# Merging neighbouring VectorE instructions of a frequency-domain mixer, and moving its bias transposes and its gelu table

## The chip, the cores and the metric

The kernel runs on one core of one Trainium2 chip. A core has TensorE (PE in the profile, with its weight loads as PEld), VectorE (DVE), ScalarE (ACT), GpSimd (POOL), and SyncE (SP), which here only issues transfers. The engines run their own instruction streams in order and meet through semaphores. The metric is the device time of one execution in microseconds (us). Before the change it is 179.74 us, the median of three runs (179.69 to 180.02).

## The reference, cut to what matters

Two branches are computed from the same input x = A_q (2048 positions, 640 channels), and a gate per position mixes them:

```python
g = sigmoid((x * gate_w).sum(-1))
# branch a: causal convolution over the 2048 positions, by FFT of length 4096
kv = (k shifted by 4 taps, weighted with shift_k) * v
y  = irfft(rfft(kv, 4096) * rfft(ssm_k, 4096))[:2048] + kv * ssm_D
a  = x * y
# branch b: a token MLP
h  = layernorm(x)
u  = gelu(h^T @ w1 + b1)        # 640 x 1536
b  = (u @ w2 + b2)^T            # 2048 x 640
return g * a + (1 - g) * b
```

Everything is bf16 in memory; matmuls accumulate in f32.

## The kernel before, in words

**The branches as engine work.** The transform of length 4096 is done as matmuls of 128x128 blocks (table FTB) on four residue classes of positions, and then VectorE "mixing": sums and differences of whole spectrum slots. A slot is 128 partitions x 2560 elements (`SL`, real part in the first 1280, imaginary in the last). Tiles C0 to C3 hold four slots each, SS two, tm0 and tm1 two each, and q_hi two (it lies on the memory of the tap table KF, and the gate's scratch gq lies on its second half). The filter's spectrum (W) and the spectrum of kv (A) are built in halves; `mixing` and `mixing_acc` (line 1092) finish them. Then `cross` (line 1229) and `product` (line 1189) multiply the spectra, with part of each sum left to a GpSimd-issued accumulating transfer ("accum" in `dma`, line 256), `invmix` (line 1241) undoes the mixing, and `inverse` (line 1263) transforms back with matmuls, scales on ScalarE with the gate (tile cgb), and multiplies with x on VectorE (q_hi holds x of the first half by then). The MLP is 12 column tiles `ft` of 32 matmuls (m1, rhs X, gelu to GT on ScalarE) and 16 output tiles of 24 matmuls (m2, rhs GT). The gate needs x * gate_w summed: VectorE multiplies (lines 1129 to 1133, tile gq), ScalarE sums with an accumulating Copy ("gsum"), and one accumulating Copy of gate_w itself ("gws", line 1128), whose unused element-wise output goes into gq[1].

**What sets the order.** A list scheduler (`_Sched.run`, line 389) with rough costs fixes, while the program is built, one order over all instructions; each engine then runs its share of that order strictly in sequence. `_Tracker` adds the waits: an instruction waits for every earlier instruction or transfer whose memory it overlaps, also where it only overwrites what another has read or written. A matmul group owns one of four PSUM slots until ScalarE has read it.

**The places that matter later, in VectorE's order before.** Times are those of the profiled execution.

- 57.92: the 5120-element difference of `mixing` for the filter's second half; 60.65 first gate product (half of hk 0, 1280 elements); 61.39 two sums of `mixing`; 64.19 the last kv product (kv1, second half), which the A matmuls at 66.50 read; 65.59 two more of `mixing`; 68.39 second gate product; 69.13 to 83.08 `mixing` of A.
- 83.08 gate product; 83.81 first difference of `mixing_acc` (slots 0 and 2); gate product; 86.09 first `cross` piece; 88.22 second difference of `mixing_acc` (slots 1 and 3, whose last ScalarE write ends at 87.55); gate products at 89.62 (two) and 92.56 (two), with `cross` pieces between and around them.
- 98.02 the third T1 product of `cross`; 100.24 the gate's last small steps behind ScalarE's tanh; the rest of `cross` up to 111.92, with the four sums of `mixing_acc` among it.
- 111.92 first `late` product into q_hi; 121.97 second `late` product into the other half of q_hi; the remaining products up to 142.38.
- 142.38 `invmix` of the first half of positions (Z0); its result for the first matmuls of `inverse` is the fifth of its eight instructions, started at 148.0.
- 153.72 to 162.27: the four x products of `inverse` (153.72, 155.86, 158.00, 160.13) alternate with the first four instructions of the second `invmix` (Z1); the fifth, which the matmuls of the second `inverse` read first, starts at 162.27.

The bias transposes are `consts` (line 853): five tiny matmuls that turn b1 and b2, loaded as rows, into columns, and a ScalarE copy to tile cc. They stand after the third W group on TensorE. The lines quoted here are the whole of them with the gelu that reads cc:

```python
act(cc[:, :], lambda s: s[:, 0:28], ACT.Copy, vt=vt, name="cc")
g_ = act(GT[:, ft, :]..., two, ACT.Gelu_apprx_tanh, bias=cc[:, 16 + ft:17 + ft], vt=vt, prio=0, name="gelu")
```

## Time and profile before

| what | value |
|---|---|
| median of three runs | 179.74 us (179.69 to 180.02) |
| span of the profiled execution | 178.7 us, first to last instruction |
| what lies around the span | 1.04 us, if that execution took the median; its own time is not listed apart |
| TensorE busy | 170.9 us (96%), clock granted 0.999 |
| VectorE busy | 169.5 us (95%), 203 instructions |
| ScalarE busy | 117.0 us (65%) |
| GpSimd busy | 43.1 us (24%) |
| moved by transfers | 43.51 MB |

A line of a timeline gives start, duration, engine, source line, operation, output and inputs, a count where like ones are merged, and in brackets how long the engine had been idle and what ended that. A group's line gives the count, the busy time with the mean of one in ns, and the idle time before. Almost every VectorE instruction carries the same source line, that of a helper, so groups are told apart by shape.

### The profile page before, as it was taken

Reading aid. Unit: us, or ns where it says so; the run is one execution under the profiler, and the core shown is the slowest. Engines: PE = TensorE matmul, PEld = TensorE weight load, DVE = VectorE, ACT = ScalarE, POOL = GpSimd, SP = SyncE. Lnnn points to the kernel's source line nnn. Section 1 sums busy time; section 2 is a strip of 40 time slices with the busy share of each in tenths; the row PEclk is TensorE's granted clock in tenths of the full one; section 3 lists DMA queues with packets and bytes.
Section 4 is the critical chain, followed back from the end, with each engine's and each line's share of the span. In section 5 each row is a group of like instructions: output and inputs, shape, how many; then the busy total and the mean of one; then the engine's idle time right before and its main releaser. Section 6 shows DMA issues by size and latency. Waiting matters only on the chain.

```text
span 178.7 us, 3326 instructions
## 1 busy us (share of the span) xinstructions
PE 170.9 (96%) x1373; PEld 128.4 (72%) x1374; DVE 169.5 (95%) x203; ACT 117.0 (65%) x176; POOL 43.1 (24%) x52
## 2 busy tenths in 40 slices
PE   7868999899999999999999999999999999999993
PEld 2545787487778677776777778888888887777772
DVE  7799889979999999999999899999999999999984
ACT  4998997999899999428999921131231323753760
POOL 8099803100000065000241100403525000252000
PEclk9999999999999999999999999999999999999999
DMA  5999999999999999999499989797999999599463
GB/s 145 384 413 372 388 301 206 264 421 299 213 258 289 189 272 235 229 229 231 97 244 285 173 132 363 158 229 241 171 194 221 208 201 394 205 164 236 114 233 138
DMA packets 38542, 43.51 MB, mean 243 GB/s; under 512 B 15867, under 2 KB 31360, under 8 KB 38528
## 3 DMA queue, kind: packets, MB, share of 16 engines
q1 hardware_dynamic: 33296, 32.16, 59.1%
q0 software_dynamic: 5200, 11.14, 35.8%
q8 instruction: 11, 0.18, 0.4%
q14 instruction: 3, 0.02, 0.0%
q10 hardware_dynamic: 32, 0.01, 0.0%
HBM read 25.87 MB, written 2.62 MB: 159 GB/s over the span
## 4 chain that ended last, share of the span: by engine, by line
PE 88%; DMA 6%; ACT 3%; SPq 2%; issue 0%; DVE 0%
PE pp L298 88%; DMA rows<-in_B_b_dram 6%; SPq L272 2%; ACT C L676 1%; ACT L676 1%; ACT GT L676 0%; DVE O L688 0%
## 5 line engine op out<-in xcount | busy, mean ns | idle before, releaser
L632 DVE TENSOR_TENSOR C<-C 128x2560 bf16<-128x2560 bf16 (+2 forms) x37 | 54.5, 1525 | 1.1 <-ACT C L676 1.1
L298 PE MATMUL pp<-X,ring 128*128 128x320 bf16 x384 | 55.4, 299 | 0.0
L298 PE MATMUL pp<-GT,W 128*128 128x320 bf16 x384 | 52.6, 299 | 0.0
L298 PEld LDWEIGHTS pp<-GT,W 128*128 128x128 bf16 x384 | 43.6, 114 | 8.6
L298 PEld LDWEIGHTS pp<-X,ring 128*128 128x128 bf16 x384 | 37.3, 98 | 14.3
L676 ACT ACTIVATE C<-pp 128x640 bf16<-128x640 f32 x64 | 40.5, 737 | 3.2 <-PE pp L298 3.2
L676 ACT ACTIVATE O<-pp,c,omg 128x640 bf16<-128x640 f32 x15 | 13.3, 884 | 34.7 <-PE pp L298 34.7
L267 POOL DMA_DIRECT2D C<-C x8 | 11.0, 1615 | 45.0 <-DVE C L632 45.0
L298 PE MATMUL pp<-wT,FTB 128*128 128x320 bf16 x112 | 17.1, 299 | 1.4 <-ACT wT L676 0.8
L676 ACT ACTIVATE cgb<-pp,gg 128x640 bf16<-128x640 f32 x16 | 12.7, 794 | 5.7 <-PE pp L298 5.3
L676 ACT ACTIVATE GT<-pp,cc 128x640 bf16<-128x640 f32 x12 | 9.6, 801 | 9.0 <-PE pp L298 9.0
L298 PEld LDWEIGHTS pp<-wT,FTB 128*128 128x128 bf16 x112 | 10.5, 98 | 6.5 <-ACT wT L676 1.2
L945 DVE BATCH_NORM_STATS2 stats<-X 128x6 f32<-128x320 bf16 x32 | 13.5, 461 | 1.1 <-DMA X<-in_A_q_dram 1.1
L632 DVE TENSOR_TENSOR tm<-C,C 128x2560 bf16<-128x2560 bf16 (+1 forms) x7 | 14.3, 2060 | 0.0
L298 PE MATMUL pp<-C,FTB 128*128 128x320 bf16 x96 | 13.4, 299 | 0.0
L267 POOL DMA_DIRECT2D C<-q_hi x6 | 5.9, 977 | 27.6 <-DVE C L632 13.1
L298 PEld LDWEIGHTS pp<-C,FTB 128*128 128x128 bf16 x96 | 9.3, 98 | 3.8 <-issue 0.2
L676 ACT ACTIVATE gq<-gq 128x640 bf16<-128x640 bf16 x16 | 11.8, 739 | 0.1
L632 DVE TENSOR_TENSOR SS<-C 128x2560 bf16<-128x2560 bf16 x8 | 11.7, 1488 | 0.1
L632 DVE TENSOR_TENSOR C<-tm 128x2560 bf16<-128x2560 bf16 (+1 forms) x9 | 10.7, 1194 | 0.1
L676 ACT ACTIVATE ksh<-pp 128x1024 bf16<-128x1024 f32 (+1 forms) x12 | 9.9, 903 | 0.2 <-PE pp L298 0.2
L676 ACT ACTIVATE wT<-pp 128x1024 bf16<-128x1024 f32 x10 | 9.7, 1027 | 0.6 <-PE pp L298 0.6
(77 smaller groups left out, 188.8 us busy)
## 6 DMA issues: line engine op xcount, KB each, us to landing
ring<-in_B_w_dram SPq DMA_DIRECT2D x12, 512.0 KB, 9.6
W<-in_B_w_dram SPq DMA_DIRECT2D x12, 512.0 KB, 6.3
C<-C POOLq DMA_DIRECT2D x8, 640.0 KB, 10.6
X<-in_A_q_dram SPq DMA_DIRECT2D x4, 640.0 KB, 9.0
kn<-in_A_k_dram SPq DMA_DIRECT2D x4, 640.0 KB, 9.3
out_dram<-O SPq DMA_DIRECT2D x7, 320.0 KB, 3.2
C<-SS POOLq DMA_DIRECT2D x3, 640.0 KB, 11.7
ssm<-in_A_ssm_k_dram SPq DMA_DIRECT2D x3, 512.0 KB, 7.4
```

Of the source, the lines that this page charges most:

```text
L267: ins = engobj.dma_start(out_ap, in_ap, accum_op=ALU.add, max_dma_last_dim=2560)
L272: ins = engobj.dma_start(out_ap, in_ap)
L298: ins = self.nc.tensor.matmul(ps_ap, lhsT=lhsT, rhs=rhs, start=start, stop=stop, skip_group_check=True)
L632: o_ = SC.add(eng, d, lambda s: T.op(eng, lambda e: e.tensor_tensor(o, a, b, op), rd, [o]), rd, [o], prio=prio, name="tt")
L676: return T.op("ACT", lambda e: e.activation(o, src, func, **kw), rr + [src], ww)
L945: ops.append(SC.add("DVE", 0.38, (lambda o, i: lambda s: T.op("DVE", lambda e: e.bn_stats(o, i), [i], [o]))(o, i), [i], [o]))
```

## The change

**Merged instructions.** C, SS and tm become windows of one tile AR of 22 slots, so that one access pattern can reach slots of two tiles. With that:

- `mixing_acc`: the two differences of 2560 elements become one of 5120; both accumulating transfers come after it.
- gate products: two of 1280 per hk become one of 2560, on one gq tile of four rows in place of two tiles of two; gws writes its output to row 2 of it.
- `cross`: per spectrum half, two passes of four instructions on single slots become four instructions on slot pairs, and two transfers of 320 KB one of 640 KB, issued before the last subtraction. One half uses the first half of q_hi, the other the second.
- the two calls of `product` for A1 become `product2`: one `late` product of 5120 elements over all of q_hi, its two transfers, one product of 10240, and two of 5120.
- `invmix`: the first four instructions of 2560 become two of 5120.

VectorE has 21 instructions fewer (182 for 203), and GpSimd two transfers fewer.

**Moved.** The bias transposes go from behind the third W group to behind the third group of m1 matmuls, and the copy to cc from behind the second W evacuation to behind the last wT copy of the second half. A new one-element gelu follows on ScalarE, reading a constant.

**The order.** The scheduler is replaced by a recorded order and recorded PSUM slots. Decoded, TensorE's order differs in the bias transposes alone, ScalarE's in cc and the new gelu, SyncE's not at all, GpSimd's in the two transfers that are gone; the PSUM slots are those of before. A merged VectorE instruction stands at one place, and this gives in the changed stretches:

```
before                                              after
237 238 | kv1 | 239 240  with gate 0a ahead,        237 238, gate 0 (2560), kv1, 239 240
  gate 0b behind (237..240: sums of mixing)
gate 1a, mixing_acc 0/2, gate 1b, gpre,             gate 1 (2560), gpre, mixing_acc (5120),
  cross pieces of the first half with               gate 2 (2560), gate 3 (2560),
  mixing_acc 1/3, gates 2a 2b 3a 3b among them      cross first half: T1, q_hi, V.re, [gth], V.im
[tanh] gg omg c2 among cross pieces                 gpre, [tanh] gg omg c2
cross second half with the four sums of             T1, two sums, q_hi, two sums, V.re, V.im
  mixing_acc among it
late, T0, im, re; T0, late, im, re                  late (5120), T (10240), im (5120), re (5120)
Z0: add add sub sub, then four                      Z0: add (5120), sub (5120), then four
x0, Z1add, x1, Z1sub, x2, Z1add, x3, Z1sub          x0, x1, x2, Z1add (5120), x3, Z1sub (5120)
then Z1's last four                                 then Z1's last four
```

`x0` to `x3` are the x products of `inverse` for the first half of positions. The core of the diff:

```diff
-                        if d not in vt.first.deps:
-                            vt.first.deps.add(d)
+                        vt.first.hint.add(d)
...
-        C = [alloc(f"C{i}", [128, 4, 4, D], BF16) for i in range(4)]
-        SS = alloc("SS", [128, 2, 4, D], BF16)
-        E_base = cur[0]
+        AR = alloc("AR", [128, 22, 4, D], BF16)
+        SS, C, tm = Win(AR, 0), [Win(AR, 2 + 4 * i) for i in range(4)], [Win(AR, 18), Win(AR, 20)]
+        E_base = cur[0] = base_of(tm[0])
...
-        gq = [alloc(f"gq{i}", [128, 2, D], BF16, at=base_of(Drow) + 5120 + 2560 * i) for i in range(2)]
+        gq = alloc("gq", [128, 4, D], BF16, at=base_of(Drow) + 5120)
...
                 consts()
+                act(gws[:, 0:1], cst[:, 1:2], ACT.Gelu_apprx_tanh, name="table").dur = 1.4
...
+            tt("DVE", sl(Th, Ts, 2), sl(R, 0, 2), sl(R, 2, 2), ALU.subtract)
             for i in range(2):
-                tt("DVE", sl(Th, Ts + i), sl(R, i), sl(R, 2 + i), ALU.subtract)
                 dma(pr(R, i), pr(R, 2 + i), 128 * 5120, stream="POOL", prio=0, accum=True)
...
-                act(gq[1][:, 0, :], gwb[:, :], ACT.Copy, acc=gws[:, :], name="gws").after.add(g_)
+                act(gq[:, 2, :], gwb[:, :], ACT.Copy, acc=gws[:, :], name="gws").after.add(g_)
...
-                for a in range(2):
-                    gb = gq[a]
-                    tt("DVE", gb[:, :, :], X[:, hk, 2 * a:2 * a + 2, :], V(gwb, 0, [[0, 2], [1, D]]), ALU.mult)
-                    for b in range(2):
-                        t = 4 * hk + 2 * a + b
-                        act(gb[:, b, :], gb[:, b, :], ACT.Copy, acc=gacc[:, t:t + 1], name="gsum")
+                tt("DVE", gq[:, :, :], X[:, hk, :, :], V(gwb, 0, [[0, 4], [1, D]]), ALU.mult)
+                for b in range(4):
+                    t = 4 * hk + b
+                    act(gq[:, b, :], gq[:, b, :], ACT.Copy, acc=gacc[:, t:t + 1], name="gsum")
...
         def cross(g):
...
+            tmp = V(q_hi, 2560 * g, [[1280, 2], [1, 1280]])
+            tt("DVE", P2(T1), P2(A0[g]), P2(V1[g], True), ALU.mult)
+            tt("DVE", tmp, H(A0[g], 1), H(V1[g], 1), ALU.mult)
+            tt("DVE", H(V1[g], 0), H(A0[g], 0), H(V1[g], 0), ALU.mult)
+            dma(H(V1[g], 0), tmp, 128 * 5120, stream="POOL", prio=0, accum=True)
+            tt("DVE", H(V1[g], 1), H(T1, 1), H(T1, 0), ALU.subtract)
+
+        def product2(a, v, into):
...
+            tg = {1: T0, 0: T1}
+            late = V(q_hi, 0, [[2560, 2], [1280, 2], [1, 1280]])
+            tt("DVE", late, Hg(a, 1), Hg(v, 0), ALU.mult)
+            for n_, g in enumerate((1, 0)):
+                dma(H(into[g], 1), V(q_hi, 2560 * n_, [[1280, 2], [1, 1280]]), 128 * 5120, stream="POOL", prio=0, accum=True)
+            tt("DVE", Pg(tg), Pg(a), Pg(v), ALU.mult)
+            tt("DVE", Hg(a, 1), Hg(a, 0), Hg(v, 1), ALU.mult)
+            tt("DVE", Hg(a, 0), Hg(tg, 0), Hg(tg, 1), ALU.subtract)
...
-            for (hy, sy), k in (((hb, sb), 1), ((ha, sa), 0)) if bfirst else (((ha, sa), 0), ((hb, sb), 1)):
-                tt("DVE", sl(hs, ss + k), sl(hy, sy), sl(hy, sy + 1), ALU.add)
-                tt("DVE", sl(hy, sy), sl(hy, sy), sl(hy, sy + 1), ALU.subtract)
+            a0, b0, s0 = slot_of(Ya), slot_of(Yb), slot_of(sc)
+            yo = [[(b0 - a0) * SL, 2], [1, SL]]
+            y0, y1 = V(AR, a0 * SL, yo), V(AR, (a0 + 1) * SL, yo)
+            tt("DVE", V(AR, s0 * SL, [[SL, 2], [1, SL]]), y0, y1, ALU.add)
+            tt("DVE", y0, y0, y1, ALU.subtract)
...
-        chained(product, A1[1], A1[1], V0[1], tmp_of(q_hi, 0), V1[1])
-        chained(product, A1[0], A1[0], V0[0], tmp_of(q_hi, 1), V1[0])
+        chained(product2, A1, V0, V1)
...
-        SC.run()
+        SC.follow([int(i) for i in _ORDER.split()], [int(i) for i in _SLOTS])
```

## The prediction

> **What bounds the kernel now.** First the page's busy line, then the chain that ended last, in order of time (start, duration, what):

> ```profile
> PE 170.9 (96%) x1373; PEld 128.4 (72%) x1374; DVE 169.5 (95%) x203; ACT 117.0 (65%) x176; POOL 43.1 (24%) x52
> ```

> ```profile
> 31.18 1.30 ACT C L676 x2
> 32.48 0.02 issue
> 32.50 1.28 ACT L676
> 33.78 0.01 issue
> 33.80 0.79 ACT GT L676
> 34.59 1.20 ACT C L676 x2
> 35.79 0.14 issue
> 35.92 140.11 PE pp L298 x1128
> ```

> From 35.92 to 176.03 us TensorE never waits. Its last input ends the kernel. So the time can fall only by what starts that run earlier, and it rises by every stall put into it. VectorE is as full as TensorE, so what matters is how late each of its results may be. Second, the VectorE groups by shape, for prices:

> ```profile
> L632 DVE TENSOR_TENSOR C<-C 128x2560 bf16<-128x2560 bf16 x27 | 39.1, 1489 | 0.0
> L632 DVE TENSOR_TENSOR C<-C 128x5120 bf16<-128x5120 bf16 x4 | 11.3, 2822 | 0.0
> L632 DVE TENSOR_TENSOR gq<-X,gwb 128x1280 bf16<-128x1280 bf16 x8 | 6.5, 826 | 0.1
> ```

> (2822 - 1489) / 2560 is 0.52 ns an element, which leaves 0.155 us fixed per instruction. Starts of neighbours lie 0.08 us closer than durations: 0.74, 1.40, 2.74 us for 1280, 2560, 5120 elements; 10240 gives 2.82 + 2.67 = 5.49, so 5.41. Third, timelines at the places where a merged instruction meets a supplier:

> ```profile
> 34.97 1.11 POOL L1079 COPY KT<-KT 128x20 bf16<-128x20 bf16 x1 [4.98 <-DMA KT<-kp]
> ...
> 63.74 0.79 ACT L676 ACTIVATE gq<-gwb 128x640 bf16<-128x640 bf16 x1
> 64.37 0.25 ACT L676 ACTIVATION_READ_ACCUMULATOR gq<-gwb 128x1 f32 x1
> 66.50 0.98 PE L298 MATMUL pp<-kv,FTB 128*128 128x320 bf16 x6
> 86.84 0.70 ACT L676 ACTIVATE C<-pp 128x640 bf16<-128x640 f32 x1
> 113.70 1.20 POOL L267 DMA_DIRECT2D C<-q_hi  x1 [1.28 <-DVE q_hi L632]
> 149.67 8.86 PE L298 MATMUL pp<-C,FTB 128*128 128x320 bf16 x64
> 158.36 5.60 PE L298 MATMUL pp<-GT,W 128*128 128x320 bf16 x40
> 163.91 4.51 PE L298 MATMUL pp<-C,FTB 128*128 128x320 bf16 x32
> ```

> The reader sees when tap data is complete (34.9), when the gws sum has written gq (64.62), when A's last evacuation is done (87.55), a transfer out of q_hi, and the two starts of the inverse.

> **The change part by part.** All times are those of this execution, span 178.7; the median of the runs is 1.04 above it.

> *What it saves.* 21 instructions fewer at 0.155 us: 3.3 us of VectorE, 19 of them (2.95 us) before Z0. None of it is time by itself, since TensorE does not wait for VectorE now. Two GpSimd issues less cost or gain nothing: its queue idles before each.

> *Bias transposes and table.* TensorE waited 0.68 us at 14.14 for the bias rows, so the W groups come about 1 us earlier. But the second m1 group (24.78) needs X tiles normalised at 24.71, behind k's landing at 23.15: this gain ends there. From there the five transposes add 0.3 us at 27.9, less 0.13 us of slack: W at 29.25 for 29.08. The new gelu moves the 1.28 us table load to about 28.5, where ScalarE idled 0.88 us, and it catches up by 32.7. Then nothing holds TensorE after the m1 group at 32.88 (8 matmuls at 0.136 us end it at 33.97, four W matmuls at 34.51, plus 0.17 us), and the taps' matmuls could start at 34.7 in place of 35.92. They need the KT transfers, complete at 34.91: start 34.97, gain **0.95 us**. Ends: 0 (the table load hits ScalarE elsewhere) and 0.95, the cap by KT; I take the cap, as every input but KT is in time. VectorE gains the same: its 1.05 us idle before 37.00 waited for ScalarE.

> *Gate product 0 behind gws.* The merged product overwrites row 2 of gq, so it waits for the gws sum: 64.62 - 0.95 = 63.67. VectorE would be free at 62.50 (56.97 + 2.74 + two of 1.40): idle 1.2 us. The kv product queued behind it starts at 63.70 + 1.40 = 65.10 and ends at 66.59. TensorE arrives at 66.50 - 0.95 = 65.55 and starts at 66.65: stall 1.1, the front's gain is spent, TensorE is **0.15 us late** from here. VectorE too (239 at 66.50, `mixing` at 69.30 for 69.13).

> *mixing_acc in one.* After gate 1 (83.08 + 0.17 = 83.25, to 84.65) and gpre (84.8), the merged difference needs all eight evacuations, 87.55 + 0.15 = 87.70: idle 2.9 us. Before, slots 0 and 2 went first, and `cross` and a gate product filled this gap. It runs to 90.46. Both its transfers now start then, not at 85.6 and 90.3; at a median 10.6 us and 1.2 more for the second they land by 102.5, and their readers, the four sums, come at 106.8: covered, by 4 us.

> *One gq tile.* Gate 2 runs 90.46 to 91.94. Gate 3 overwrites the same rows, so it waits for four sums on ScalarE (90.49 to 93.47 before, 2.98 us): 94.95. Idle 3.05 us; two tiles hid this. Gate 3 then ends its slot at 96.40.

> *cross and the gate's small steps.* T1 2.74, q_hi 1.40, V.re 1.40, gth 0.08, V.im 1.40, gpre: 103.6. ScalarE's tanh (0.24 with its hand-over) is no longer covered by the next T1: 103.85, and the small steps end at 104.1, where `cross`'s second half starts; 98.02 before. ScalarE's later gelus do not stop TensorE: four PSUM slots rotate, and the next users of theirs come at 106 or later.

> *late behind the transfer.* T1, two sums, q_hi, two sums and V.re end at 115.33. The transfer out of q_hi's second half is issued 0.3 us later, and `late` now overwrites all of q_hi, so it waits for the landing. The two of this size took these times (the second line is the range over all that touch q_hi):

> ```profile
> C<-q_hi POOLq DMA_DIRECT2D x2, 640.0 KB, 6.2
> ...
> DMA to landing us min/median/max: 3.6/5.5/9.0
> ```

> 115.63 + 6.2 = 121.85: idle 5.05 us behind V.im (ends its slot at 116.8). Ends 3.6 and 9.0; I take 6.2, the same size, queue and tile. Queued behind `late` is the whole rest of VectorE. `product2`: 2.74, 5.41, 2.74, 2.82 to 135.6; the next product started at 126.54, so **9.06 us late**.

> *Z0.* The next 15.84 us are unchanged: add at 151.44. It needs the accumulating transfer out of SS, issued at 132.72 and landed at 142.77 before (SyncE's q_hi load, which waits for it, is at 142.79), so now at 151.83. Add 2.82, sub 2.74, first sum 1.49 and 0.15 of hand-over (163.76 to 163.91 before): TensorE starts the inverse at **159.1**, having been there at 149.82. Idle 9.3 us. SyncE's q_hi load starts 9 us late too and lands 8 to 9.3 us after 151.83, by 161.1; x0 needs it at 163 and is not held.

> *A cold array.* No row shows TensorE after such an idle. Nearest rows: after at most 0.85 us nothing happens; after none at all, the first seven 512-column matmuls start 0.43 us apart and later ones 0.215. That lasted 3.1 us (1.18 to 4.27), at half rate a loss of 1.55. Ends 0 and 1.55; I take 1.55, since 9.3 us is ten times the harmless gap. The granted clock reads 1.00 in both stretches and does not tell. [...]

> *Z1.* Counted from the start T of the first inverse, TensorE arrives at the second at T + 14.24 (163.91 - 149.67). x2 needs the cgb evacuation that ended at 157.18: T + 7.58. Behind it, in order: x2 0.74, add 2.74, x3 0.74, sub 2.74, the first sum 1.49, hand-over 0.15: T + 16.2. Before, Z1's instructions filled the waits between the x products, and ended at 163.76. **Stall 1.95 us**, whatever T is. The second inverse's own products and the output transfers follow it as before.

> *Sum.* 159.1 + 16.2 + 1.55 = 176.85 for 163.91; then as before, 178.7 - 163.91 = 14.79: span 191.65, with 1.04 **192.7 us**, 12.95 more.

> **The rivals.** *Nothing is held (faster):* if VectorE's new idle time before Z0 stayed under the 2.95 us saved, and x2 were fed 1.95 us earlier, only the front would count: 179.74 - 0.95 = **178.8**. The place is the merged instructions between 62 and 122; it decides below 2.95 us, and I count 12.6 (1.2, 2.9, 3.05, 0.35, 5.05). For it speaks that VectorE shows almost no idle now, so slack on its suppliers is not visible; against it that each supplier's end is in a row above.

> *Only the end counts:* the mid-kernel waits are mostly absorbed, Z0 in time, and Z1's 1.95 stays with the 0.15: **181.8**; with the q_hi wait gone alone (a landing before 116.8) 192.7 - 5.05 = **187.6**. For it: 320 KB landed in 3.6 once. Against it: 5.2 to 6.2 are the medians.

> *The array stays warm:* **191.1**. For it: the granted clock never fell; against it, the start.

> *More than counted:* landing at 9.0 (+2.8) and a cold second inverse (+1.55): **197.0**.

> **How the numbers follow.** Forecast with its own bounds, 188.5 (192.7 - 2.6 for a 3.6 landing - 1.55 for a warm array) to 197.0: 0.76, warm array included (0.25 of it). Partly absorbed, 181.8 to 188.5: 0.13, of which half lies above 186. Faster: 0.05. Above 197: 0.05. No change: 0.01, where front gain and stalls cancel. The range 186 to 197 leaves out about 0.18. A measurement of this kernel tells apart about 0.2%, the spread of its runs (0.36 us). Faster 0.05, same 0.02, slower 0.93.

> **What would show it.** Right: VectorE idle about 3 us before the 5120-element difference near 87.7, 3 us before the last gate product, 5 us before the product into q_hi, named as waits for ScalarE twice and for the transfer once; TensorE idle about 9 us before the first C,FTB matmuls and about 2 us before the second lot; twice the usual 0.136 us between those matmuls' starts for some 3 us; taps' matmuls at 35.0. Wrong: TensorE still unbroken to the end, or the idle times sitting elsewhere, for example on ScalarE's table load.

## The result, and the profile after

The changed kernel takes **194.88 us** (median of seven executions, 194.39 to 197.77) where the kernel before takes 179.94 (seven, 179.54 to 180.40): a ratio of 1.083, 95% interval 1.081 to 1.085. It is 14.9 us slower; 12.95 was forecast.

The execution that was profiled took 197.58 us with a span of 195.3; it is one of two among the seven in which TensorE's granted clock was low for longer (means of 0.965 and 0.956) than in the other five (0.973; 194.4 to 195.4 us), so what it shows behind 160 us is some 2.7 us too long for the median, while its clock reads 1.00 up to 155 us.

First the page's busy line and its row of the granted clock, in 40 slices:

```profile
PE 176.0 (90%) x1373; PEld 129.7 (66%) x1374; DVE 169.0 (87%) x182; ACT 117.4 (60%) x177; POOL 44.1 (23%) x50
PEclk9999999999999999999999999999999855998899
```

VectorE has 21 instructions fewer and is almost as busy as before (169.0 for 169.5 us, its products having moved to longer instructions at the same rate: 2560 elements take 1.486 us for 1.489, and 5120 take 2.821 for 2.822), but 87% of a longer span where it was 95%. The clock row falls to 5 from 156 to 166 us: in the last part of the stretch in which TensorE is idle, and in the work right behind it.

The chain that ended last, in order of time (start, duration, what), from the tap table on:

```profile
28.08 6.66 DMA KT<-kp
34.78 23.76 PE pp L298 x267
...
63.58 1.49 DVE gq L552
65.07 1.41 DVE kv L552
66.61 15.39 PE pp L298 x112
...
87.76 2.83 DVE AR L552
...
92.02 3.00 ACT gq L596 x8
...
115.84 6.85 DMA AR<-q_hi
122.81 2.82 DVE q_hi L552
125.64 5.42 DVE AR L552
...
159.99 9.28 PE pp L298 x48
```

Before, this chain was one TensorE piece of 140 us. Now it leaves TensorE three times: ahead of 66.61 for ScalarE's gws sum and the gate product that waits for it, from 82 to 159.99 for ScalarE and VectorE, and again between the two inverses. For those 78 us this chain does not pass through TensorE. The waits of VectorE and TensorE by length in total (who waited for whom: us, times, longest):

```profile
PE pp L298 <- DVE AR L552: 12.0, 2, 10.0
DVE q_hi L552 <- DMA AR<-q_hi: 5.9, 1, 5.9
DVE gq L552 <- ACT gq L596: 4.2, 2, 3.1
DVE AR L552 <- ACT AR L596: 2.9, 1, 2.9
```

VectorE's three lines are the four waits that the merging made: `late` into q_hi behind a transfer out of it (5.9), gates 0 and 3 behind ScalarE's readers of the same rows (1.1 and 3.1), the merged `mixing_acc` behind A's last evacuation (2.9). TensorE's line is its two idle times ahead of the inverses, 10.0 and 1.96 us; the second comes from Z1's place behind the third x product. Its timeline (start, duration, what, count, idle before):

```profile
66.61 0.97 PE L298 MATMUL pp<-kv,FTB 128*128 128x320 bf16 x6 [1.13 <-DVE kv L552]
...
159.99 11.44 PE L298 MATMUL pp<-AR,FTB 128*128 128x320 bf16 x64 [10.04 <-DVE AR L552]
171.27 5.60 PE L298 MATMUL pp<-GT,W 128*128 128x320 bf16 x40
178.82 10.53 PE L298 MATMUL pp<-AR,FTB 128*128 128x320 bf16 x64 [1.96 <-DVE AR L552]
```

The first inverse started at 149.67 before. Its 64 matmuls, 8.86 us then, take 11.44. And the prices of the merged shapes, from the groups by shape (count, busy, mean ns, idle before):

```profile
L552 DVE TENSOR_TENSOR AR<-AR 128x2560 bf16<-128x2560 bf16 x40 | 58.0, 1486 | 0.3
L552 DVE TENSOR_TENSOR AR<-AR 128x5120 bf16<-128x5120 bf16 x16 | 45.1, 2821 | 3.1 <-ACT AR L596 2.9
L552 DVE TENSOR_TENSOR AR<-AR 128x10240 bf16<-128x10240 bf16 x1 | 5.5, 5484 | 0.0
```

### The profile page after: what moved, and what is told of

It reads as the page before. It is cut to its first block, busy times and chain, and to the rows that moved or that the text cites. A ratio compares the mean times of both kernels' runs of the same rounds, so it can differ in the third digit from the quotient of the medians.

```text
span 195.3 us, 3307 instructions
## 1 busy us (share of the span) xinstructions
PE 176.0 (90%) x1373; PEld 129.7 (66%) x1374; DVE 169.0 (87%) x182; ACT 117.4 (60%) x177; POOL 44.1 (23%) x50
## 4 chain that ended last, share of the span: by engine, by line
DVE 38%; PE 38%; ACT 12%; DMA 7%; issue 4%; POOL 0%; DVEq 0%; POOLq 0%
PE pp L298 38%; DVE AR L552 28%; ACT AR L596 4%; DMA AR<-q_hi 4%; DMA KT<-kp 3%; DVE q_hi L552 3%; ACT wT L596 2%; ACT gq L596 2%; ACT FTB L596 2%; DVE gq L552 2%; DVE stats L865 1%; DVE kv L552 1%; DVE X L567 0%; ACT cgb L596 0%; DVE kp L684 0%
## 5 line engine op out<-in xcount | busy, mean ns | idle before, releaser
L552 DVE TENSOR_TENSOR AR<-AR 128x2560 bf16<-128x2560 bf16 (+3 forms) x63 | 112.4, 1825 | 3.5 <-ACT AR L596 2.9
L298 PE MATMUL pp<-X,ring 128*128 128x320 bf16 x384 | 55.8, 299 | 0.0
L298 PE MATMUL pp<-GT,W 128*128 128x320 bf16 x384 | 52.6, 299 | 0.0
L298 PEld LDWEIGHTS pp<-GT,W 128*128 128x128 bf16 x384 | 43.5, 113 | 8.7
L298 PEld LDWEIGHTS pp<-X,ring 128*128 128x128 bf16 x384 | 37.1, 98 | 14.8 <-DVE X L567 0.6
L596 ACT ACTIVATE AR<-pp 128x640 bf16<-128x640 f32 x64 | 40.4, 733 | 3.3 <-PE pp L298 3.2
L596 ACT ACTIVATE O<-pp,c,omg 128x640 bf16<-128x640 f32 x15 | 13.3, 885 | 34.4 <-PE pp L298 34.4
L298 PE MATMUL pp<-AR,FTB 128*128 128x320 bf16 x128 | 22.0, 343 | 12.0 <-DVE AR L552 12.0
L298 PEld LDWEIGHTS pp<-AR,FTB 128*128 128x128 bf16 x128 | 14.1, 111 | 19.8 <-issue 10.3
L267 POOL DMA_DIRECT2D AR<-AR x11 | 13.6, 1502 | 59.9 <-DVE AR L552 59.9
L298 PE MATMUL pp<-wT,FTB 128*128 128x320 bf16 x112 | 17.0, 299 | 0.8 <-ACT wT L596 0.8
L298 PEld LDWEIGHTS pp<-wT,FTB 128*128 128x128 bf16 x112 | 10.4, 98 | 6.0 <-ACT wT L596 1.2
L267 POOL DMA_DIRECT2D AR<-q_hi x4 | 4.8, 1326 | 30.2 <-DVE AR L552 12.3
L552 DVE TENSOR_TENSOR q_hi<-AR 128x2560 bf16<-128x2560 bf16 (+1 forms) x3 | 5.8, 1930 | 5.9 <-DMA AR<-q_hi 5.9
L267 POOL DMA_DIRECT2D O<-q_hi x4 | 4.8, 1200 | 24.5 <-DVE q_hi L552 24.5
L298 PE MATMUL pp<-KF,KT 128*128 128x128 bf16 (+1 forms) x160 | 9.1, 213 | 0.5 <-DMA KT<-kp 0.5
```

Of the source, the lines that this page charges most:

```text
L267: ins = engobj.dma_start(out_ap, in_ap, accum_op=ALU.add, max_dma_last_dim=2560)
L298: ins = self.nc.tensor.matmul(ps_ap, lhsT=lhsT, rhs=rhs, start=start, stop=stop, skip_group_check=True)
L552: o_ = SC.add(eng, d, lambda s: T.op(eng, lambda e: e.tensor_tensor(o, a, b, op), rd, [o]), rd, [o], prio=prio, name="tt")
L596: return T.op("ACT", lambda e: e.activation(o, src, func, **kw), rr + [src], ww)
```

## The experiments

The theory: merging saves VectorE nothing that counts, and each place where one instruction now needs two suppliers is a wait; the waits add up along VectorE's fixed order and reach TensorE at the two inverses, and the array, idle before, then runs cold (11.44 us for the 8.86 of before). Two rivals: long instructions over one large tile are slow as such; or only the end (Z1's place) counts and the earlier waits are absorbed. In the edits, `mv(a, b)` moves instructions of the recorded order `o` ahead of another, and `by[n]` is instruction n; the numbers are positions in the program. The comments are added here.

### Each place undone alone

**Z1's first instructions back between the x products**, still merged:

```diff
+mv([614], 597); mv([615], 604); mv([616], 611)   # Z1 add, sub, first sum: ahead of x1, x2, x3
```

> The changed kernel (194.9 us) with one thing undone: the second invmix's instructions stand between the x products again (add behind x0, sub behind x1, the first sum behind x2). Theory (each loss is a wait of one in-order VectorE instruction): the 1.96 us stall of TensorE before the second inverse goes to under 0.3 us, the 10 us stall before the first stays; 192.9 us, down to 191.3 if that stall also cost TensorE clock. Rival (the longer instructions and the one-tile layout are slow as such): within 0.5 us of 194.9.

Measured 193.19 us (192.37 to 193.68), ratio to before 1.073 (1.068 to 1.078). The second stall is gone from the trace, and nothing else changed: the first inverse starts at 160.26 after 10.08 us idle. So the end alone is 1.7 of the 14.9 us.

**The 10240-element product ahead of `late`**, so that it runs while the transfer out of q_hi lands:

```diff
+mv([560], 557)   # product of 10240 elements: ahead of late
```

> The changed kernel with the 10240-element product moved ahead of the late product into q_hi, nothing else. Theory: the 5.9 us wait of VectorE for the transfer out of q_hi is covered by 5.41 us of that product; the first inverse starts about 5.4 us earlier (154.6 for 160.0), 189.5 us. Rival (long instructions slow as such): within 0.5 us of 194.9.

Measured 190.56 us (189.56 to 193.08), ratio 1.058 (1.054 to 1.063). Of the wait for the transfer 0.3 us is left, and the first inverse starts at 155.09, 4.9 us sooner: the wait of 5.9 us was on the path nearly in full.

**The first half's `cross` back between the gate products and ahead of `mixing_acc`:**

```diff
+mv([547], 370)                        # cross, first half: T1 ahead of mixing_acc's difference
+mv([548, 549, 550, 551], 437)         # its q_hi, V.re, transfer, V.im ahead of gate 3
+mv([552], 466); mv([553], 470)        # second half: T1 ahead of gth, q_hi ahead of gg
```

> The changed kernel with VectorE's order repaired around the gate products only: the first T1 product of cross ahead of the mixing_acc difference, the rest of cross's first half between gate products 2 and 3, the second T1 ahead of gth and the second q_hi product ahead of gg. Memory and instructions are unchanged. Theory: the waits of 2.9, 3.05 and 0.3 us are filled; the first inverse starts 6.2 us earlier (153.8), 188.7 us. Rival (single gq tile costs by itself, not by order): under 1 us gained.

Measured 191.04 us (189.97 to 192.43), ratio 1.062 (1.054 to 1.070): 3.8 us for the 6.2 expected. VectorE's waits in this kernel say a part of why:

```profile
DVE q_hi L552 <- DMA AR<-q_hi: 4.6, 1, 4.6
...
DVE gg L567 <- ACT gth L596: 1.4, 1, 1.4
...
DVE gq L552 <- ACT gq L596: 0.9, 1, 0.9
```

The 6 us of waits of `mixing_acc` and gate 3 on ScalarE are gone; the 0.9 left is gate 0's for gws, which this edit does not touch. But the wait for the tanh grew from 0.3 to 1.4 us: the chain over gsum, gpre and tanh is ScalarE's, and ScalarE is no faster (a gsum takes 738 ns in the changed kernel, 739 before). And this execution was 0.6 us late already ahead of the gates (gate 0 at 64.15 for 63.58). The first inverse started at 155.20 (153.8 expected), 4.8 us sooner, and the profiled execution, 190.09 us, is 4.8 us faster than the changed kernel. The last 1.0 us of the shortfall comes with the clock: the median lies between two executions at 190.0 and 190.1 us with a mean granted clock of 0.991 and two at 192.0 and 192.4 us with 0.964 and 0.973.

**gws into another place:** the unused output goes into q_hi, so gate 0 has no reason to wait.

```diff
-act(gq[:, 2, :], gwb[:, :], ACT.Copy, acc=gws[:, :], name="gws")
+act(V(q_hi, 640, [[1, D]]), gwb[:, :], ACT.Copy, acc=gws[:, :], name="gws")
```

> The changed kernel with gws's unused output put into q_hi's first half (free then) in place of row 2 of gq. Theory: gate product 0 no longer waits 1.1 us, TensorE's 1.1 us stall before the A matmuls at 66.6 goes, and everything behind comes 1.1 us earlier: 193.8 us. Rival: another supplier (the kv product's own ScalarE input) ends just as late, under 0.3 us gained.

Measured 193.89 us (193.20 to 194.58), ratio 1.078 (1.072 to 1.083). The stall at 66.6 is gone and the first inverse starts 1.3 us sooner, at 158.68, still after 10.09 us idle: TensorE arrives as much earlier as VectorE does.

### All four undone, the merged instructions kept

> The changed kernel with all four repairs: Z1 between the x products, the long product ahead of late, the gate order, gws's output elsewhere. All merged instructions stay merged. Theory: VectorE is in time everywhere, TensorE runs unbroken from about 34.8 us on, only the front's gain is left: 178.8 us, ratio 0.994. Rival (merged instructions or layout slow as such): above 185 us. If a wait moves to a place not counted: 180 to 184.

Measured **181.55 us** (181.06 to 184.98), ratio 1.008 (1.005 to 1.011). So 13.3 of the 14.9 us are these four places, with every merged instruction, the one tile and 182 VectorE instructions kept: the rival of slow long instructions (above 185 us) is refuted as the main cause, and so is the one that the early waits are absorbed. (The four gains singly sum to 10.8. Of the 2.5 us more, some 1.75 can be the cold array: five of these six executions have a mean clock of 0.999 or 1.00, where all of the changed kernel have 0.973 or less. The rest was not traced.) But 178.8 was not reached; the expectation's third case, a wait at a place not counted, fits. The timeline of TensorE and the waits of VectorE in this kernel:

```profile
152.21 10.53 PE L298 MATMUL pp<-AR,FTB 128*128 128x320 bf16 x64 [2.29 <-DVE AR L552]
162.58 5.60 PE L298 MATMUL pp<-GT,W 128*128 128x320 bf16 x40
168.01 8.86 PE L298 MATMUL pp<-AR,FTB 128*128 128x320 bf16 x64
```

```profile
DVE AR L552 <- DMA AR<-AR: 2.2, 1, 2.2
...
DVE gg L567 <- ACT gth L596: 1.4, 1, 1.4
```

What is left is a wait of Z0's add for the accumulating transfer out of SS (VectorE reached it at 142.6, the transfer landed at 144.8), and the tanh. The last experiments take these two apart. (The 10.53 us of the first inverse are a cold array in this execution, 184.98 us, whose clock is 0.55 from 152.2 to 156 and 0.981 in the mean.)

### The cold array

In the changed kernel, unused 512-column matmuls fill TensorE's two stalls:

```diff
+nw = {(0, 0, 0): 40, (1, 0, 0): 8}.get((h, p, kt), 0)
+warm = [((lambda s: s[:, 0:512]), GT[:, 0, 0:128], GT[:, 0, 0:512], True, True)] * nw
-mms(vt, items, name="inv")
+mms(vt, warm + items, name="inv")
```

> The changed kernel with 40 unused 512-column matmuls ahead of the first inverse's first group and 8 ahead of the second's, in the PSUM slot that the group then overwrites; outputs are unchanged. Theory: TensorE's matmuls after both stalls run at 0.136 us at once; the loss to clock (1.6 us in the faster runs, 4.3 in the slower) goes, 193.3 us and no second group of runs at 197.7. Rival: the slower matmuls after the stall come from something else (operand reads beside VectorE), time unchanged.

Measured 193.13 us (192.80 to 193.39), ratio 1.073 (1.070 to 1.076): 1.75 us less than the changed kernel, with 48 matmuls more. TensorE's timeline in it:

```profile
149.97 8.58 PE L298 MATMUL pp<-GT 128*128 128x512 bf16 x39
159.89 8.87 PE L298 MATMUL pp<-AR,FTB 128*128 128x320 bf16 x64 [1.34 <-DVE AR L552]
```

The inverse starts where it did (159.89 for 159.99) and takes 8.87 us for 11.44. The clock by stretch in the changed kernel, without the filling (stretch, length, then busy time with instructions of PE, PEld, DVE, ACT and POOL, PEclk, DMA share, GB/s):

```profile
145.00:155.00 10.00, 4.94 (x37) 3.86 (x35) 9.93 (x5) 1.77 (x2) 1.64 (x2) 1.00 1.08 177
155.00:160.00 5.00, 0.01 (x1) 0.04 (x2) 4.93 (x4) 0.00 (x0) 0.00 (x0) 0.51 1.03 336
160.00:164.00 4.00, 4.00 (x16) 2.28 (x17) 3.96 (x3) 0.79 (x1) 0.00 (x0) 0.50 0.76 314
164.00:168.00 4.00, 4.00 (x26) 2.67 (x25) 1.05 (x3) 2.38 (x3) 1.20 (x1) 0.84 0.02 4
168.00:172.00 4.00, 4.00 (x32) 2.98 (x30) 2.65 (x3) 2.92 (x4) 1.96 (x2) 1.00 0.85 133
```

16 matmuls in four microseconds at a clock of 0.50, 32 at 1.00; and the clock halves at 155, while TensorE is still idle, 5.1 us after its last matmul. The rival "the array stays warm" is refuted, and so is the one of this experiment: VectorE does the same work beside the filled kernel's matmuls (3.96 us busy of the four from 160 to 164, in both kernels), and they run at full rate (31 in those four microseconds at a clock of 1.00). At a clock of 0.50 the 1.75 us lost in the execution of median time are an estimated 3.5 us of work; in the profiled one, 11.44 for 8.87 us make 5.1 us, which is longer. And an idle time of 10 us was not needed: the second inverse ran cold (10.53 us, a clock of 0.66 from 179 to 184) after 1.96 us.

### Before, with one part of the change

**Z1's three instructions behind the third x product**, nothing merged:

```diff
+for i in (634, 635, 636): o.remove(by[i])
+k = o.index(by[624]) + 1
+o[k:k] = [by[634], by[635], by[636]]
```

> The kernel before with three instructions of the second invmix moved behind the third x product, as in the changed order but unmerged. Theory: VectorE waits for the cgb evacuations with nothing to fill, TensorE stalls about 2.05 us before the second inverse: 182.0 us, up to 1.7 more if the stall costs clock. Rival (VectorE runs early enough to absorb it): 179.9.

Measured 181.96 us (181.68 to 182.63), ratio 1.011 (1.008 to 1.015), as expected without a loss of clock. The second inverse's line in it:

```profile
165.50 4.51 PE L298 MATMUL pp<-C,FTB 128*128 128x320 bf16 x32 [2.10 <-DVE C L632]
```

A change of three places in an order, with the instructions left as they were, costs the stall that was forecast for Z1 (1.95).

**The bias transposes and the gelu table alone:**

```diff
+tab = act(gws[:, 0:1], cst[:, 1:2], ACT.Gelu_apprx_tanh, name="table")
+o.remove(by[67]); o.insert(o.index(by[384]), by[67])    # transposes: behind the third m1 group
+o.remove(by[68])                                        # copy to cc and the gelu: behind the last wT copy
+k = max(o.index(by[199]), o.index(by[67])) + 1
+o[k:k] = [by[68], tab]
```

> The kernel before with the front alone: bias transposes behind the third m1 group, cc and a one-element gelu behind the last wT copy; no instruction merged, order otherwise that of before. Theory: the taps' matmuls start 1.1 us earlier, bounded by the KT transfers, and the whole run keeps it: 178.8 us, ratio 0.994. Rival: later data (X, ring, kv) is not earlier and the gain is given back: 179.9.

Measured 179.62 us (179.04 to 180.84, twelve executions) beside 180.04 for the kernel before, ratio 0.9985 (0.9962 to 1.0008): the direction is as expected, the size is under half, and the interval takes in no change. Its trace shows the step itself: the taps' matmuls start at 34.30, and TensorE's waits for C and GT ahead of them are gone. But they started at 35.92 in the profile of before and at 35.37 in that of the kernel with Z1's three instructions moved, whose front is the same. The gain was sized from one late execution; the usual one has less to win. And of the 1.07 us to the start at 35.37, 0.32 is lost again in the taps themselves, whose 72 matmuls take 4.26 us for 3.94.

### What is left: the tanh, and a queue of transfers

Both kernels start from the one with the four places undone. In the first, the three small steps behind the tanh stand one sum later:

```diff
+mv([470, 471, 472], 374)   # gg, omg, c2: behind the first sum of mixing_acc
```

> The kernel with the four repairs takes 181.55 us, 1.5 more than the kernel before. Its profile has two waits left on VectorE ahead of Z0: 1.4 us for the tanh and 2.2 us for the accumulating transfer out of SS. Here the three small steps behind the tanh stand one sum of mixing_acc later. If the waits are what is left: the tanh wait falls to about 0, all that follows on VectorE and its transfers come 1.4 us earlier, the first inverse waits 0.9 us where it waited 2.3, and the time is 180.2 us. Rival, the rest belongs to the merged instructions themselves (or to the one tile): 181.5 us. Second rival, the transfers ahead of Z0 wait in their queue and not for VectorE: the tanh wait goes, the wait for the SS transfer grows by as much, 181.5 us as well.

Measured 182.09 us (181.40 to 183.84), ratio 1.009 (1.005 to 1.012): no gain, the second rival held. The tanh wait is gone and the two transfers out of q_hi are issued at 119.72 and 120.45 where it was 121.39 and 122.12, but they land at 128.1 and 131.3 as before (128.2, 131.4), and the wait for the one out of SS grows from 2.2 to 2.8. The stretches of this kernel (the last two numbers are the share of the 16 DMA engines in use, and GB/s):

```profile
116.00:120.00 4.00, 4.00 (x31) 3.35 (x30) 3.96 (x3) 1.61 (x2) 0.28 (x1) 1.00 0.41 129
120.00:124.00 4.00, 4.00 (x32) 3.33 (x30) 3.97 (x2) 1.04 (x2) 2.16 (x2) 1.00 0.94 268
124.00:128.00 4.00, 4.00 (x31) 3.35 (x30) 3.96 (x2) 0.88 (x1) 0.00 (x0) 1.00 1.11 219
128.00:132.00 4.00, 4.00 (x32) 3.33 (x31) 3.90 (x3) 0.89 (x1) 3.08 (x3) 1.00 0.97 180
132.00:136.00 4.00, 4.00 (x31) 3.35 (x30) 4.00 (x3) 1.31 (x2) 3.02 (x3) 1.00 1.04 201
136.00:140.00 4.00, 4.00 (x32) 3.33 (x31) 3.97 (x3) 1.34 (x2) 0.00 (x0) 1.00 1.11 222
```

From 120 on the DMA engines are full, and from 116 to 120 they are at 0.41: the transfer out of q_hi ahead of these two had landed at 115.6, and `late` in one piece, now behind the 10240-element product, hands over both of its transfers only at its end. That is a price of merging which no wait of the first profile names: it bunches transfers. In the second kernel `late` alone is split again, one half ahead of the 10240-element product and one behind it, in place of moving that product:

```diff
-late = V(q_hi, 0, [[2560, 2], [1280, 2], [1, 1280]])
-tt("DVE", late, Hg(a, 1), Hg(v, 0), ALU.mult)
 for n_, g in enumerate((1, 0)):
+    tt("DVE", V(q_hi, 2560 * n_, [[1280, 2], [1, 1280]]), H(a[g], 1), H(v[g], 0), ALU.mult)
     dma(H(into[g], 1), V(q_hi, 2560 * n_, [[1280, 2], [1, 1280]]), ...)
...
-mv([560], 557)
+o = [i + (i > 558) for i in o]                           # one instruction more
+o.remove(561)                                            # the 10240-element product
+o[o.index(558) + 1:o.index(558) + 1] = [561, 559]        # then the second half of late
```

> Only the late product is split again, into its two halves of 2560 elements, the first ahead of the product of 10240 and the second behind it, each with its transfer. In the kernel with the four repairs both transfers out of q_hi start together at 121.4 and land at 128.2 and 131.4, and the five behind them land 3 to 5 us apart, so that the one out of SS lands at 144.8, 2.2 us too late for Z0. With the first issued near 115, the next transfers can start at 127 in place of 128.8: the wait of Z0 falls from 2.2 to 0.3 us, the added instruction costs 0.15 on VectorE, the first inverse waits 0.5 us, and the time is 179.8 us. Rival, the merged instructions themselves: 181.5 us or, for the added instruction, a little more.

Measured 181.03 us (179.77 to 182.53), ratio 1.002 (0.997 to 1.007). The median alone doesn't decide, but the mean granted clock of each execution sorts them: of six with 0.998 or more, five took 179.8 to 180.2 us, as expected, and one 182.1; the five with 0.981 or 0.990 took 181.0 to 182.5. The profile agrees: VectorE has no wait for a transfer there any more (the 1.4 us for the tanh are still there), and TensorE passes into the first inverse without a stall, at 150.09.

With both edits:

> Both of the two edits. If the waits are all that was left: no wait over 0.5 us for a transfer or for ScalarE between 85 and 145, TensorE comes to the first inverse later than its operand is ready, no stall there, and the time is that of the kernel before with the front alone, since TensorE has the same work in one piece: 179.6 us, 179.3 to 180.1. So it would show that the 18 merged VectorE instructions that are kept are worth nothing here, as TensorE and not VectorE sets the end. Rival, the merged instructions cost something of their own: 180.5 us or more.

Measured **179.70 us** (178.98 to 183.02, twelve executions), ratio to the kernel before beside it 0.996 (0.993 to 0.999). VectorE's longest wait between 85 and 145 us is 0.3. TensorE's timeline at the end in it:

```profile
139.71 9.94 PE L298 MATMUL pp<-GT,W 128*128 128x320 bf16 x72
149.49 8.86 PE L298 MATMUL pp<-AR,FTB 128*128 128x320 bf16 x64
158.19 5.60 PE L298 MATMUL pp<-GT,W 128*128 128x320 bf16 x40
163.62 8.86 PE L298 MATMUL pp<-AR,FTB 128*128 128x320 bf16 x64
```

In one piece again. This version beats the changed kernel by 15 us, and by its ratio the kernel before by 0.4%, with an interval that just leaves out no change; it has 183 VectorE instructions for 203. The front alone, with 203, comes to 179.62 and a ratio whose interval overlaps this one: the 20 instructions saved (the expectation's 18 is a miscount) are worth nothing that can be measured, since TensorE sets the end in both.

## Why the prediction was right, and where it was off

It said slower, 192.7 in a range of 186 to 197; 194.88 was measured. Point by point, by the profiled execution:

| step, as the prediction put it | predicted | after |
|---|---|---|
| taps' matmuls start | 34.97 | 34.78 |
| kv product behind gate 0; TensorE's stall | 65.10; 1.1 | 64.98; 1.13 |
| `mixing_acc` waits, starts | 2.9, 87.70 | 2.9, 87.76 |
| gate 3 waits, T1 starts | 3.05, 96.40 | 3.1, 96.45 |
| transfer out of q_hi: issued, landing taken | 115.63, 6.2 | 115.84, 6.85 |
| `late` starts | 121.85 | 122.81 |
| 10240-element product | 5.49 | 5.48 |
| the product behind the merged ones starts | 135.6 | 136.79 |
| Z0's add | 151.83 | 152.63 |
| first inverse; idle before it | 159.1; 9.3 | 159.99; 10.04 |
| second stall | 1.95 | 1.96 |

**Right.** Every wait stood where it was forecast, for the named reason, but a small one of 0.39 us at Z0 (below); each of the four places, undone alone, took its wait away or left at most 0.3 us of it; for two of the four the gain in time came within 0.4 us of what was expected, for the other two it fell short by 1.1 and 2.3. TensorE's first inverse came 0.89 us later than forecast. The duration of a merged instruction (0.155 us fixed, 0.52 ns an element) held to 0.01 us (5.48 for 5.49) for the 10240-element form that the trace of before did not have.

**Off, by 2.18 us.** Two terms of the sum were mis-sized, and one beside it.

- *"The median of the runs is 1.04 above it"*, what lies around the span. It took the profiled execution of before for a median one. Executions with both numbers listed show 1.8 to 2.0 for the kernel before (180.24 us with a span of 178.3, 179.38 with 177.4) and 2.2 to 2.3 for the changed one (194.88 with 192.6, 195.37 with 193.2). So the profiled execution of before was about 0.7 us above its median, and the term is 2.28 for the changed kernel: 1.24 us of the miss. Why it grew from 1.9 to 2.2 stays open; all kernels with the recorded order have it, with stalls or without.
- *Up to the first inverse*, 0.89 us in the profiled execution: `late` came 0.96 us late, 0.65 for the landing (6.85 for 6.2), 0.21 for the issue and 0.1 for the hand-over. Behind it, neighbours that depend on each other are 2.84 us apart for 5120 elements where 2.74 or 2.82 was taken, another 0.23 up to 136.79. And 0.39 came back: Z0's add was taken to wait for the transfer out of SS until 151.83, and by the trace it waited for nothing, as that transfer had landed at 149.9. That this error ran against the others is luck. The last 0.09 lies between Z0's add and the inverse, 7.36 us; the four terms there make 7.20, and the sum wrote 159.1 for 159.03.
- *"21 instructions fewer at 0.155 us: 3.3 us of VectorE"*. VectorE's busy time fell by 0.5 us, and by 0.8 in the kernel with both edits. The prediction's own starts say why: neighbours of 2560 elements start 1.40 us apart and those of 5120 2.74, so one for two saves 0.06. The eight products around `late` took 14.62 us before (111.92 to 126.54) and four took 13.98 after (122.81 to 136.79); Z0's add and sub took 5.72 in two for some 5.62 in four, since the two merged ones depend on each other and start 2.86 apart. And 17 of the 21 stand ahead of Z0's add, not 19. No part of the 192.7 uses this term, but it is the threshold of the first rival.

With the execution of median time, span 192.6, put beside the profiled one up to 160 us, 0.06 is left for the rest: 0.89 + 0.06 + 1.24 = 2.19.

**The cold array: right in kind, near in size.** 1.55 was forecast for the usual execution; the changed kernel less the filled one gives 1.75. But it is no constant. In the profiled execution the first inverse lost 2.6 us (11.44 for 8.86) and the second, after only 1.96 us idle, 1.7 more, which is what put it at 197.58, above the range. The prediction had a cold second inverse as a part of the rival "more than counted". The sentence that the granted clock does not tell was wrong for this stage: it reads 0.50.

**The front.** The start of the taps came out right, and the gain did not: it was measured from 35.92, which was that execution's own lateness by about half a microsecond. Alone it came to 0.3 us by its ratio and 0.4 by the medians, not 0.95, and the interval takes in no gain at all. It could not show in the changed kernel, where it is spent at 66.6. Nor is the start at 34.8 a constant: in the profiles of the kernel with the four places undone and of the three made from it TensorE ran at a clock of 0.50 for 3.4 us between 7.4 and 12.6 us (mean clocks of 0.981, 0.991, 0.990 and 0.990), and the taps start at 35.6 to 36.0.

**The rivals.** "Nothing is held" fell with the first wait. "Only the end counts" falls with the other three places, which gained 9.1 us between them, one at a time, beside the 1.7 of Z1's. "The array stays warm" falls with the filled stalls.

## What to carry to other kernels

Here an instruction made of two started with the later of its two suppliers (`mixing_acc` 2.9 us, `late` 5.9 us later than its engine was free) and freed its rows with the last of their readers (gate 3 waited 3.1 us), and it handed over both transfers only at its end (`late` ended at 125.63, GpSimd issued the two from 125.94 to 128.37); everything behind it in its engine's order came later, and TensorE stood idle for 10.0 us ahead of the first inverse. So a merge is priced by the slack at its place, not by what it saves: 21 merges saved 0.5 us of VectorE's busy time and none of the kernel's, and at four places they took 13.3 us. The same instructions in better places, gws's output out of the way and one merge taken back, took none. And before merging, see whether the engine sets the end at all: VectorE was 95% busy and not the bound.
